# Three changes to the loads of a decode block: where the large tiles lie, how W_o's first heads are split over the DMA engines, and how many pieces W_down comes in

## Chip, cores and metric

The kernel runs on one core of a Trainium2 chip. The metric is the time of one execution on the device, in microseconds. One execution is also profiled; its span runs from the first to the last instruction of the program.

## What is computed

One decode step of a transformer block for B = 2 sequences: layer norm, attention over a cache, and a gated MLP. All tensors are bf16.

```python
D, Hq, Sk, Dh, F = 512, 32, 8192, 128, 1376        # x: [2, 1, 512]
q = layernorm(x) @ wq                              # 32 heads of 128
p = softmax(einsum("bhqd,bhkd->bhqk", q, k_cache) * Dh ** -0.5)
o = einsum("bhqk,bhkd->bhqd", p, v_cache)          # k_cache, v_cache: [2, 32, 8192, 128]
h = x + o.reshape(2, 1, 4096) @ wo
g, u = layernorm(h) @ W_gate, layernorm(h) @ W_up  # [512, 1376]
out = h + (relu(g) * u) @ W_down
```

The caches are 2 x 134 MB and make up nearly all of the 281 MB that are read.

## The kernel before

**Tiles.** Three large buffers (L90, tile0 to tile2) of 64 KB in each of the 128 partitions take turns as K and V tiles. A step (class Step, L130) covers four heads of one sequence: its K tile and its V tile are 8 MB each, loaded by one DMA of 128 rows of 64 KB (load_tile, L160). There are 15 such steps; the last four heads are done as two steps of two heads each (p0, p1), with tiles of half the size. wq lies in half of tile2 at the start. At the end W_o goes into the upper half of tile0 (wo, L125), W_gate and W_up into tile2 (wgu, L126) and W_down into tile1 (wd_sb, L127). The pool `front` stands ahead of the buffers and holds qTs and ocol; all small tiles follow behind them in `consts`.

**A step.** For most of the cache rows DVE multiplies the K tile by q (products, L378) and folds the 128 products of a row in halves (scores, L396, then L398). For the others PE transposes K (L352), ACT copies it back (L353) and PE multiplies by q (L343). DVE finds the maximum (L402 to L417), ACT takes the exponentials (L418), DVE puts them into pgq (L423), and PE multiplies them by the V tile (values, L449).

**Order.** The order on each engine is that of the code (`manual_schedule`). All large loads are issued by SP and go through one queue, which spreads each over the 16 DMA engines; a 128-row load gives every engine 8 rows. A load is issued once its buffer is free, and once the load eight before it has landed, since eight semaphores take turns.

**The end.** After the last full step SP issues V of p0, W_o's first 16 heads (load_set(0), L569, issued from L573), V of p1 in four pieces (L588), W_o's other heads by loads of 8, 4 and 2 heads and the last two (L589 to L594), W_gate and W_up in two pieces each (L614) and W_down (L619). SETS (L68) lists W_o's loads by head: in a load of n heads each partition takes n * D elements in one run. FSETS (L73) does this for W_down by chunks of 128 rows of F: a piece of n chunks gives each partition n * D elements in one run. PE multiplies the heads' output by W_o (attend_set, L505, and attend, L512), then comes the layer norm, then gate and up (through, L673, whose weights are read with a step of n elements in a piece of n chunks), DVE's product (L708), and W_down (L712), chunk by chunk in the order of the loads. The result is transposed (L721), copied (L722) and stored (L723).

Of the kernel before, what the change touches and what calls it, by code (L numbers as in the profile page):

```python
# [13 lines left out]
def _free(t, offset, dims):  # L14

    return bass.AP(tensor=t.tensor, offset=t.offset + offset, ap=[t.ap[0]] + [list(d) for d in dims])


def _dram(t, offset, dims):
    return bass.AP(tensor=t.tensor, offset=t.offset + offset, ap=[list(d) for d in dims])  # L20
# [3 lines left out]
def kernel(  # L24
# [13 lines left out]
    nc = tc.nc  # L38
    P = nc.NUM_PARTITIONS
    B, Sq, D = A_x.shape  # L40
    _, Hkv, Sk, Dh = A_k_cache.shape
    Hq = A_wq.shape[1] // Dh
    F = B_W_gate.shape[1]
# [3 lines left out]
    bf16 = mybir.dt.bfloat16  # L47
    f32 = mybir.dt.float32
# [3 lines left out]
    NQ = Hq // NH  # L52
# [14 lines left out]

    SETS = [(0, 16, 0), (16, 8, 16), (24, 4, 24), (28, 2, 28)]  # L68
    HM = 30
    SROWS = [n for _, n, _ in SETS]  # L70


    FSETS = [(0, 3), (3 * P, 3), (6 * P, 1), (7 * P, 1), (8 * P, 1), (9 * P, 1), (F - P, 1)]  # L73
    FC = 11
    AGAIN = 32

# [3 lines left out]
    front = ctx.enter_context(tc.tile_pool(name="front", bufs=1))  # L80
    big = ctx.enter_context(tc.tile_pool(name="big", bufs=1))
    consts = ctx.enter_context(tc.tile_pool(name="consts", bufs=1))
# [3 lines left out]

    qTs = front.tile([P, B, Hq], bf16)
    ocol = front.tile([P, Hq, B], bf16)

    bufs = [big.tile([P, TILE], bf16, name=f"tile{k}") for k in range(3)]  # L90

# [4 lines left out]
    pv = consts.tile([P, VG * Dh], f32)  # L96
    pick = consts.tile([P, VG, 4, NH], f32)
    zc = consts.tile([P, B, NQ, NH], f32)
    zs = consts.tile([P, B, NQ], f32)
    own = consts.tile([P, NH], f32)  # L100
    ownb = consts.tile([P, NH, VG], bf16)
    ecol = consts.tile([P, TILE // Dh], bf16)
    qzp = consts.tile([P, 2, 16], bf16)
    qz = consts.tile([P, 2 * QZ], bf16)
    ident = consts.tile([P, P], bf16)
    ident_f = consts.tile([QZ, QZ], f32)
# [5 lines left out]
    hm = consts.tile([P, FC, B], bf16)  # L112
    quot = {r: consts.tile([P, Dh // r], bf16, name=f"quot{r}") for r in SROWS}
    rest = {r: consts.tile([P, r], bf16, name=f"rest{r}") for r in SROWS}
    orow = [consts.tile([P, r, B], bf16, name=f"orow{k}") for k, r in enumerate(SROWS)]
    sel = consts.tile([B, B, P // 2], bf16)
# [8 lines left out]
    wo = bufs[0][:, HALF:TILE]  # L125
# [43 lines left out]
    def ln_cols(src, dst_bkc, pfx):  # L169

        m_ps = ps.tile([P, B, KC], f32, tag="mx")
        nc.tensor.matmul(out=m_ps, lhsT=mean_w, rhs=src, start=True, stop=True)
        mean = small.tile([P, B], f32, tag=pfx + "mean")
        nc.vector.tensor_reduce(out=mean, in_=m_ps, axis=AXIS.X, op=ALU.add)
        dev = small.tile([P, B, KC], f32, tag=pfx + "dev")
        nc.vector.tensor_tensor(out=dev, in0=src, in1=_free(mean, 0, [[1, B], [0, KC]]), op=ALU.subtract)
        sq = small.tile([P, B, KC], f32, tag=pfx + "sq")
        nc.vector.tensor_tensor(out=sq, in0=dev, in1=dev, op=ALU.mult)
        v_ps = ps.tile([P, B, KC], f32, tag="mx")
        nc.tensor.matmul(out=v_ps, lhsT=mean_w, rhs=sq, start=True, stop=True)  # L180
        rstd = small.tile([P, B], f32, tag=pfx + "rstd")
        nc.vector.tensor_reduce(out=rstd, in_=v_ps, axis=AXIS.X, op=ALU.add)
        nc.scalar.activation(out=rstd, in_=rstd, func=ACT.Sqrt, bias=eps_col, scale=1.0)
        nc.vector.reciprocal(out=rstd, in_=rstd)
        nc.vector.tensor_tensor(out=dst_bkc, in0=dev, in1=_free(rstd, 0, [[1, B], [0, KC]]), op=ALU.mult)

    with tc.manual_schedule():
# [11 lines left out]
            out=nscale, in_=nscale, compare_op=ALU.not_equal, fill=-SCALE,  # L199
# [5 lines left out]
            out=ident_f, in_=ident_f, compare_op=ALU.not_equal, fill=1.0,  # L205
# [4 lines left out]
            out=sel, in_=sel, compare_op=ALU.not_equal, fill=1.0,  # L210
# [9 lines left out]
            out=pick, in_=pick, compare_op=ALU.not_equal, fill=1.0,  # L220
# [17 lines left out]
        ln_cols(xc, xn.rearrange("p c b -> p b c"), "l1")  # L238
        for r in SROWS:
            nc.vector.tensor_reduce(out=rest[r], in_=_free(ident, 0, [[1, r], [r, P // r]]), axis=AXIS.X, op=ALU.max)  # L240
# [4 lines left out]
        for g0 in range(0, NQ, 4):  # L245
            for n0 in range(NH * g0 * Dh, NH * (g0 + 4) * Dh, 4 * Dh):
                q_ps = ps2.tile([B, 4 * Dh], f32, tag="o")
                for c in range(KC):
                    nc.tensor.matmul(  # L249
                        out=q_ps, lhsT=xn[:, c, :], rhs=wq_sb[:, c, n0:n0 + 4 * Dh], start=(c == 0), stop=(c == KC - 1),  # L250
                    )
                nc.vector.tensor_copy(qrow[:, n0:n0 + 4 * Dh], q_ps)  # L252
            for b in range(B):
                r_ps = ps2.tile([P, 4, Dh], f32, tag="tp")
                for j in range(NH):
                    nc.tensor.matmul(
                        out=r_ps[j * (P // NH):(j + 1) * (P // NH)], lhsT=sel[:, b, 0:P // NH],
# [5 lines left out]
        for j in range(2):  # L263
            nc.tensor.matmul(
                out=r_ps[j * (P // 2):(j + 1) * (P // 2)], lhsT=sel[:, B - 1, :],
# [224 lines left out]
        def lay_rows(k, sps, scalar=False):  # L490

            r = SROWS[k]
            or_ps = ps.tile([P, B, r], f32, tag="mx")
# [7 lines left out]
        def attend_set(k, r0=0, r1=None):  # L501
            for c0 in range(r0, SROWS[k] if r1 is None else r1):
                for c in range(KC):
                    at = (SETS[k][2] + c0) * D + c
                    nc.tensor.matmul(  # L505
                        out=att_ps[:, c, :], lhsT=_free(wo, at, [[KC, P]]), rhs=orow[k][:, c0, :],
                        start=(k == 0 and c0 == 0 and c == 0), stop=False, skip_group_check=True,
                    )

        def attend(h):  # L510
            for c in range(KC):
                nc.tensor.matmul(  # L512
                    out=att_ps[:, c, :], lhsT=_free(wo, h * D + c, [[KC, P]]), rhs=ocol[:, h, :],
                    start=False, stop=(h == Hq - 1), skip_group_check=True,
                )
# [50 lines left out]
        own_sums(Q)  # L566
        def load_set(k):
            h0, n, at = SETS[k]
            nc.sync.dma_start(  # L569
                out=wo[:, at * D:(at + n) * D], in_=_dram(A_wo, h0 * Dh * D, [[n * D, P], [1, n * D]]),  # L570
            )

        load_set(0)  # L573
        products(p0, p0.na)

        at = [0, 0]
# [12 lines left out]
        for k in range(1, len(SETS)):  # L589
            load_set(k)  # L590
        nc.sync.dma_start(
            out=wo[:, HM * D:Hq * D].rearrange("p (h n) -> p h n", n=D),
            in_=_dram(A_wo, HM * Dh * D, [[D, P], [Dh * D, Hq - HM], [1, D]]),
        )  # L594
# [18 lines left out]
        for w, src, c, n in ((0, B_W_gate, 0, 2), (0, B_W_gate, 2, 2), (1, B_W_up, 0, 2), (1, B_W_up, 2, 2)):  # L613
            nc.sync.dma_start(  # L614
                out=wgu[:, w, c:c + n].rearrange("p c f -> p (c f)"), in_=_dram(src, c * F, [[KC * F, P], [1, n * F]]),
            )
        for f0, n in FSETS[-1:] + FSETS[:-1]:
            fc = FC - 1 if f0 == F - P else f0 // P
# [7 lines left out]
            out=z2_ps, lhsT=ones, rhs=_free(zc, ((B - 1) * NQ + groups[Q][1]) * NH, [[1, nb]]), start=True, stop=True,  # L626
# [19 lines left out]
        for k in range(1, len(SETS)):  # L646
            attend_set(k)
        for h in range(HM, Hq):
            attend(h)
# [15 lines left out]

        chunks = [(f0 + c, n) for f0, n in FSETS for c in range(n)]
        UP = 6
# [13 lines left out]
        for c in range(KC):  # L681
# [10 lines left out]
            out=gate, in0=g_ps, scalar=0.0, in1=_free(rvar, 0, [[0, FC], [1, B]]), op0=ALU.max, op1=ALU.mult,  # L692
# [7 lines left out]
        for c in range(KC):  # L700
            nc.tensor.matmul(
                out=d_ps[:, c, :], lhsT=hrow[:, c * P:(c + 1) * P], rhs=ident_f[0:B, 0:B],
# [7 lines left out]
        for fc in order:  # L710
            for c in range(KC):
                nc.tensor.matmul(  # L712
                    out=d_ps[:, c, :], lhsT=wd_sb[:, fc, c * P:(c + 1) * P], rhs=hm[:, fc, :],
# [40 lines left out]
```

## Time and profile before

| | us |
|---|---|
| median of 3 runs | 662.56 |
| lowest and highest of them | 661.42 and 663.75 |
| the profiled execution | 661.14 |
| its span | 659.3 |

The head of the profile gives the busy time of the engines in that span: DVE 557.4 us (85%), PE 353.1 (54%), ACT 122.9 (19%), POOL 7.6 (1%). The 16 DMA engines moved 281.40 MB, 427 GB/s in the mean. "Queue 1" is the one that SP's loads go through; queues 8 and 14 bring instructions. In a row of the timeline the first number is the start in us from the span's start, the second the length; what stands in brackets is the time that the engine had been idle, and what ended it. The chain of waits is the work that ended last, followed backwards from the last instruction. The trace also has a record of each DMA packet, with start, length, size and queue; one row of a load is one packet.

### The profile page before, as it was taken

How to read it: one execution, taken by the hardware profiler on the slowest of the kernel's cores; microseconds unless marked ns; L12 is line 12 of the kernel's file. 1: busy time of each engine (PE TensorE's matmuls, PEld its weight loads, DVE VectorE, ACT ScalarE, POOL GpSimd, SP SyncE). 2: the span in 40 equal slices, each digit the busy share in tenths (PEclk: the TensorE clock that was granted, in tenths of full speed). 3: DMA queues.
4: the chain of work that ended last, by engine and by line, in shares of the span. 5: the costliest groups of instructions: out<-in, count | busy, mean ns of one | idle time of the engine just before them, and what ended most of it. 6: DMA issues, size and time to landing. Idle time of an engine off the chain costs nothing.

```text
span 659.3 us, 5118 instructions
## 1 busy us (share of the span) xinstructions
PE 353.1 (54%) x2123; PEld 160.8 (24%) x2123; DVE 557.4 (85%) x248; ACT 122.9 (19%) x335; POOL 7.6 (1%) x35
## 2 busy tenths in 40 slices
PE   3540924709174480917438092562909358291987
PEld 1220311304022130402214041220403224030456
DVE  2399697989979699997979979896997969999981
ACT  1130030301103020020302102030210304201870
POOL 3000000000000000000000000000000000000010
PEclk9865875959778595977859687695968869686985
DMA  9999999999999999999999999999999999999997
GB/s 382 445 442 445 433 399 441 441 446 434 414 433 430 441 438 421 433 437 426 441 425 434 437 426 433 421 442 437 425 434 427 437 438 425 437 430 412 426 414 279
DMA packets 7946, 281.40 MB, mean 427 GB/s; under 512 B 882, under 2 KB 1780, under 8 KB 2804
## 3 DMA queue, kind: packets, MB, share of 16 engines
q1 hardware_dynamic: 7920, 281.09, 99.0%
q8 instruction: 16, 0.26, 0.2%
q14 instruction: 6, 0.05, 0.0%
q10 hardware_dynamic: 4, 0.00, 0.0%
HBM read 281.09 MB, written 0.00 MB: 426 GB/s over the span
## 4 chain that ended last, share of the span: by engine, by line
DVE 47%; DMA 34%; PE 17%; ACT 1%; issue 1%; SPq 0%; DVEq 0%; ACTq 0%
DMA tile<-in_A_k_cache_dram 28%; DVE tile L378 21%; DVE tile L396 20%; PE pv_ps L449 16%; DMA tile<-in_A_v_cache_dram 3%; DVE scol L398 3%; DMA tile<-in_B_W_up_dram 2%; DVE pgq L423 1%; DMA tile<-in_B_W_down_dram 1%; ACT ecol L418 1%; DVE pm L402 1%; DVE qrep L398 0%; DVE pm L413 0%; DVE hmax L415 0%; PE z_ps L308 0%
## 5 line engine op out<-in xcount | busy, mean ns | idle before, releaser
L449 PE MATMUL pv_ps<-tile,pgq 128*16 128x512 bf16 x960 | 241.8, 417 | 236.4 <-DVE pgq L423 225.0
L378 DVE TENSOR_TENSOR tile<-tile,qrep 128x29696 bf16<-128x29696 bf16 (+3 forms) x16 | 232.4, 14522 | 37.7 <-DMA tile<-in_A_k_cache_dram 37.7
L396 DVE TENSOR_TENSOR tile<-tile 128x14848 bf16<-128x14848 bf16 (+7 forms) x68 | 236.5, 3477 | 2.3
L449 PEld LDWEIGHTS <-pgq 128*16 128x16 bf16 x960 | 91.0, 97 | 376.4 <-DVE pgq L423 235.1
L353 ACT ACTIVATE tile<-t_ps 128x1024 bf16<-128x1024 bf16 x53 | 52.5, 1022 | 18.6 <-PE t_ps L352 18.2
L454 ACT ACTIVATE pv<-pv_ps 16x512 f32<-16x512 f32 (+1 forms) x16 | 9.4, 589 | 234.0 <-PE pv_ps L449 233.9
L418 ACT ACTIVATE ecol<-scol,nmax 128x256 bf16<-128x256 f32 x14 | 7.1, 508 | 196.7 <-DVE nmax L417 196.7
L352 PE MATMUL t_ps<-ident,tile 128*128 128x128 bf16 x424 | 32.7, 230 | 18.1 <-DMA tile<-in_A_k_cache_dram 18.1
L343 PE MATMUL row_ps<-tile,qz 128*24 128x512 bf16 (+1 forms) x98 | 31.0, 399 | 18.6 <-ACT tile L353 18.5
L352 PEld LDWEIGHTS <-tile 128*128 128x128 bf16 x424 | 26.1, 103 | 33.3 <-DMA tile<-in_A_k_cache_dram 18.7
L398 DVE TENSOR_REDUCE scol<-tile 128x232 f32<-128x1856 bf16 (+1 forms) x14 | 28.9, 2067 | 0.5
L423 DVE TENSOR_TENSOR pgq<-ecol,ownb 128x1024 bf16<-128x1024 bf16 x15 | 10.4, 692 | 10.3 <-ACT ecol L418 10.3
L384 ACT ACTIVATE tile<-tile 128x128 bf16<-128x128 bf16 x60 | 17.6, 295 | 1.9 <-DVE tile L378 1.9
L378 DVE TENSOR_TENSOR tile<-tile,qpair 128x4096 bf16<-128x4096 bf16 (+3 forms) x4 | 15.5, 3882 | 0.0
L343 PEld LDWEIGHTS <-qz 128*24 128x24 bf16 (+1 forms) x98 | 7.9, 93 | 28.7 <-issue 23.5
L249 PE MATMUL q_ps<-tile,xn 128*2 128x512 bf16 x32 | 9.7, 469 | 8.4 <-DMA tile<-in_A_wq_dram 8.4
L252 DVE CAST tile<-q_ps 2x512 bf16<-2x512 f32 x8 | 5.4, 678 | 10.2 <-PE q_ps L249 10.2
L370 ACT ACTIVATE scol<-sc_ps 32x24 f32<-32x24 f32 (+1 forms) x56 | 11.7, 209 | 7.7 <-PE sc_ps L365 7.2
L365 PE MATMUL sc_ps<-ident_f,tile 24*128 24x24 f32 (+2 forms) x68 | 7.2, 220 | 11.0 <-ACT tile L361 11.0
L361 ACT ACTIVATE tile<-row_ps 24x512 f32<-24x512 f32 (+2 forms) x17 | 10.0, 586 | 13.4 <-PE row_ps L343 13.4
L312 DVE RECIPROCAL rz<-z_ps 128x16 f32<-128x16 f32 (+1 forms) x4 | 0.9, 236 | 13.1 <-PE z_ps L308 13.1
L384 ACT ACTIVATION_READ_ACCUMULATOR tile<-tile 128x1 f32 x60 | 11.3, 188 | 0.0
(130 smaller groups left out, 132.9 us busy)
## 6 DMA issues: line engine op xcount, KB each, us to landing
tile<-in_A_k_cache_dram SPq DMA_DIRECT2D x2, 4096.0 KB, 22.8
tile<-in_A_wq_dram SPq DMA_DIRECT2D x1, 4096.0 KB, 12.1
tile<-in_A_v_cache_dram SPq DMA_DIRECT2D x1, 4096.0 KB, 19.7
tile<-in_A_v_cache_dram SPq DMA_DIRECT2D x4, 1024.0 KB, 21.0
tile<-in_A_wo_dram SPq DMA_DIRECT2D x1, 2048.0 KB, 24.2
tile<-in_B_W_gate_dram SPq DMA_DIRECT2D x2, 688.0 KB, 13.8
tile<-in_B_W_up_dram SPq DMA_DIRECT2D x2, 688.0 KB, 12.9
tile<-in_A_wo_dram SPq DMA_DIRECT2D x1, 1024.0 KB
```

The costliest lines, as they stand in the source:

```text
L343: nc.tensor.matmul(out=row_ps, lhsT=z, rhs=s.kt[:, (nv + c0 + k) * Dh:(nv + c0 + k + 4) * Dh], start=(u == 0), stop=(u == U - 1),)
L352: nc.tensor.transpose(t_ps[:, k, :], s.kt[:, t * Dh:(t + 1) * Dh], ident)
L353: nc.scalar.activation(out=s.kt[:, (nv + c0) * Dh:(nv + c0 + TPC) * Dh], in_=t_ps.rearrange("p t s -> p (t s)"), func=ACT.Copy,)
L361: nc.scalar.activation(out=rows, in_=row_ps, func=ACT.Copy)
L370: nc.scalar.activation(out=scols[s.i][r, nv:s.nt].rearrange("p (u t) -> p t u", t=4), in_=sc_ps[r, :, :, j], func=ACT.Copy,)
L378: nc.vector.tensor_tensor(out=kv, in0=kv, in1=_free(s.qr, 0, [[0, n], [1, Dh]]), op=ALU.mult)
L384: nc.scalar.activation(out=kv, in_=kv, func=ACT.Copy, accum_out=scols[s.i][:, t:t + 1])
L396: nc.vector.tensor_tensor(out=lo, in0=lo, in1=hi, op=ALU.add)
L398: nc.vector.tensor_reduce(out=scol[:, s.na:s.nv], in_=_free(s.kt, s.na * Dh, [[Dh, s.nv - s.na], [1, 8]]), axis=AXIS.X, op=ALU.add,)
L418: nc.scalar.activation(out=ecol, in_=scols[s.i], func=ACT.Exp, scale=SCALE, bias=nmax, accum_out=zs[:, s.b, s.g:s.g + 1],)
L423: nc.vector.tensor_tensor(out=s.pg, in0=_free(ecol, 0, [[VG, s.nt // VG], [0, NH], [1, VG]]), in1=_free(ownb, 0, [[0, s.nt // VG], [VG, NH ...
L449: nc.tensor.matmul(out=pv_ps[s.i][r, :], lhsT=s.pg[:, u].rearrange("p j t -> p (j t)"), rhs=s.vt[:, u * VG * Dh:(u + 1) * VG * Dh], start= ...
```

## The change

The diff, whole:

```diff
     SETS = [(0, 16, 0), (16, 8, 16), (24, 4, 24), (28, 2, 28)]
     HM = 30
+    P4 = 16
+    LEVEL = 1
     SROWS = [n for _, n, _ in SETS]
...
-    FSETS = [(0, 3), (3 * P, 3), (6 * P, 1), (7 * P, 1), (8 * P, 1), (9 * P, 1), (F - P, 1)]
+    FSETS = [(0, 4), (4 * P, 3), (7 * P, 1), (8 * P, 1), (9 * P, 1), (F - P, 1)]
...
     qTs = front.tile([P, B, Hq], bf16)
     ocol = front.tile([P, Hq, B], bf16)
+    zs = front.tile([P, B, NQ], f32)
+    qzp = front.tile([P, 2, 16], bf16)
...
-    zs = consts.tile([P, B, NQ], f32)
...
-    qzp = consts.tile([P, 2, 16], bf16)
...
         def load_set(k):
             h0, n, at = SETS[k]
+            w = n * D
+            if k < LEVEL:
+                nc.sync.dma_start(
+                    out=wo[0:P4, at * D:(at + n) * D],
+                    in_=_dram(A_wo, h0 * Dh * D, [[P4 // 4 * w, 4], [w, P4 // 4], [1, w]]),
+                )
+            r0 = P4 if k < LEVEL else 0
             nc.sync.dma_start(
-                out=wo[:, at * D:(at + n) * D], in_=_dram(A_wo, h0 * Dh * D, [[n * D, P], [1, n * D]]),
+                out=wo[r0:P, at * D:(at + n) * D], in_=_dram(A_wo, h0 * Dh * D + r0 * w, [[w, P - r0], [1, w]]),
             )
```

It has three parts. The small tiles zs and qzp move into the pool ahead of the three large buffers, which then start 128 bytes further on in each partition, at a multiple of 512 bytes. The load of W_o's first 16 heads becomes two: partitions 0 to 15 by a load whose DRAM side is written as four groups of four rows, and so is spread over four engines, and partitions 16 to 127 by one that all 16 engines share. W_down comes in six pieces instead of seven, of 4, 3, 1, 1, 1 chunks and the last one, where it had 3, 3, 1, 1, 1, 1 and the last one; the last is still loaded first.

## The prediction

> **What bounds the kernel now.** I read the page's head first (spans, queues), then the DVE rows of the timeline from 499 us on, then the PE rows of the tail, then the chain of waits at its end, and last the single DMA packets.
>
> The page: the span, the share in which the 16 DMA engines were busy, and the queues.
>
> ```profile
> span 659.3 us, 5118 instructions
> ...
> DMA  9999999999999999999999999999999999999997
> ...
> q1 hardware_dynamic: 7920, 281.09, 99.0%
> q8 instruction: 16, 0.26, 0.2%
> q14 instruction: 6, 0.05, 0.0%
> ```
>
> The loads never stop: queue 1 alone holds the engines 99.0% of the span. The trace's packet records (start, length and size of each) can be put into sixteen chains, one per engine, by matching each start to an earlier end. On every chain one row follows the other without a gap from 1.75 us to the end of W_down, except where an instruction fetch (q8, 16 KB) stops one engine for about 1.0 us, and makes its next row 0.47 us longer, or a q14 packet stops one for 0.3 us. So the DMA bounds the run, and the engine that had most fetches ends each load last. At the end of W_o's first load the sixteen ends are 627.10, 627.23, 627.32, 627.55, 627.80, then six from 628.38 to 628.84, then five from 629.60 to 629.93: five ahead by 2.1 us or more, five last. W_down's rows end between 652.0 and 655.72.
>
> Is DMA time at the end worth its face? DVE's timeline (start, length, engine, line; in brackets the idle time before and what ended it):
>
> ```profile
> 499.62 15.09 DVE L378 TENSOR_TENSOR tile<-tile,qrep 128x28672 bf16<-128x28672 bf16 x1 [4.19 <-DMA tile<-in_A_k_cache_dram]
> ...
> 538.35 0.26 DVE L312 RECIPROCAL rz<-z_ps 128x16 f32<-128x16 f32 x1 [4.13 <-PE z_ps L308]
> ...
> 573.87 14.55 DVE L378 TENSOR_TENSOR tile<-tile,qrep 128x27648 bf16<-128x27648 bf16 x1
> ...
> 610.53 5.48 DVE L378 TENSOR_TENSOR tile<-tile,qpair 128x10240 bf16<-128x10240 bf16 x1
> ...
> 636.88 0.85 DVE L398 TENSOR_REDUCE qrep<-tile 128x84 f32<-128x672 bf16 x1
> ```
>
> DVE waits for a load for the last time at 499.6 us. From there it works on to 638.1 (131.3 busy of 138.5 us), stopped only by PE and ACT. PE takes over:
>
> ```profile
> 645.36 2.01 PE L505 MATMUL att_ps<-orow,tile 128*128 128x2 bf16 x56
> ...
> 648.94 1.59 PE L673 MATMUL g_ps<-hn,tile 128*128 128x2 bf16 x44 [0.46 <-DVE hn L660]
> ...
> 654.95 1.53 PE L712 MATMUL d_ps<-hm,tile 128*128 128x2 bf16 x44 [0.26 <-DVE hm L708]
> ```
>
> None of its idle times names a load. And the chain of waits, end (start, length, what):
>
> ```profile
> 650.86 5.30 DMA tile<-in_B_W_down_dram
> 656.16 0.05 issue
> 656.21 0.28 PE d_ps L712 x4
> ```
>
> The last four matmuls of L712 start at 656.209; the one before started at 655.989, and they follow each other every 27 ns: PE waited 0.19 us for W_down. So two chains end within 0.2 us of each other: the loads, and compute that hangs on the K tile of 499 us. What the loads win after 499 us is worth 0.19 us at most. What they lose is paid almost in full: W_gate's second piece ends at 648.42, and from W_down the landing is seen 0.44 us after the last row (655.72 to 656.16), so it is there at 648.86, while L673 wants it some 50 ns after 648.94.
>
> **Part 1: tiles at multiples of 512 bytes.** The built program places tile0 at byte 16768 of a partition, 384 past a multiple of 512; zs and qzp (64 bytes each) go in front and make it 16896. Nothing is added on an engine; in the built programs PE, DVE, ACT and POOL have the same instructions in the same order, and only SP's loads differ. A row of 64 KB starts 2414 ns after the one before, one of 8 KB (W_o) after 306, one of 1 KB after 42 to 43. So a byte costs (2414 - 306) / 57344 = 0.03676 ns, and a row has 4.7 to 4.9 ns that do not grow with its size. That surplus is all that alignment could take. Of rows whose tile address differs there are W_gate's and W_up's four pieces, at 384, 256, 128 and 0 bytes past a multiple of 512: all have 207 ns from row to row. Three undisturbed 8 KB packets of q14, an instruction queue that writes no tile, took 309 ns, as most 8 KB rows of V and W_o did. Bounds: nothing, or 4.7 ns a row, 8 + 25 x 8 = 208 rows before the K tile of 499 us, 0.98 us; as a loss, one more such surplus, the same. I take nothing, since the four pieces speak for it.
>
> [...]
>
> **Part 2: W_o's first 16 heads in two loads.** Before, each engine takes 8 rows of 16 KB, 610 ns each. After, partitions 0 to 15 go as 4 x 4 rows through four engines, the other 112 as 7 rows through each: four engines take 11 rows (+1.83 us), twelve take 7 (-0.61). If the four are among those ahead, they end at 627.55 + 1.83 = 629.38 at the latest, the others at 629.93 - 0.61 = 629.32: the last end comes 0.55 earlier, and with it every later load. The chains that started first stayed among those ahead, but no record names an engine. Worth: 0.19 us, the wait of PE; then W_down is no longer late, L712 itself is. If the four are not the ones ahead: +1.83 at worst. The second issue costs SP 0.33 to 0.43 us at 606.2, where it next waits until 611.96, so nothing. Each issue waits for the landing of the eighth before it; with one more in the row, the 8-head load waits for the second K half instead of the first (about 615.6), the 4-head load for V's first half (625.5), and the next two for the two new loads (by 630.4 as now). All run only after 637, so they stay hidden.
>
> **Part 3: W_down in six pieces.** 8 rows of the 56 per engine fall away, and one completion packet: 8 x 4.7 + 9 = 47 ns, inside the 0.19. SP issues one less (0.33 us), and the last piece waits for W_gate's second piece instead of W_up's first, so earlier. PE meets W_gate and W_up with a step of 4 for four chunks, where it had 3 for three: L505, with a step of 4, needs 33 ns a matmul, L712 with none 27, and one more chunk is 8 matmuls: at most 0.05 us. Chunk 3 now comes with chunks 0 to 2, which were there by 653.8, and is wanted after 655.
>
> **Sum.** 0 - 0.19 (parts 2 and 3 together, capped by PE) + 0.05 at most: -0.15 to -0.2 us. The profiled execution took 661.14 us (span 659.3 and 1.8 around it), 1.4 less than the median of the three runs, 662.56. So 660.9 against itself, and 662.4 against the median, which I give. About 0.3% (2 us) is what a measurement of this kernel can tell from no change.
>
> **Rivals.**
> - *The surplus is the address.* The K tile of 499 lands 0.98 earlier, DVE's chain starts as much earlier, the loads end further ahead: -0.98 - 0.19 = -1.2, 661.4. For it: the surplus doesn't grow with the row, as the cost of a bad start would not. Against: 207 ns four times.
> - *Slower: the 112 rows cross.* The sixteen engines take seven consecutive partitions each, so they no longer keep to the partitions that each has in a load of 128. If two engines that write into partitions with a common way into the tile share its rate, a row takes 2 x 0.61. None of seven doubled gives -0.61, all seven +3.66; with five of seven on the last engine it ends 3.05 - 0.61 = 2.4 later, at 632.3, W_gate, W_up and W_down follow, and PE meets each late: 662.56 + 2.4 = 665.0. It decides from the second doubled row on the last engine. Against: x's two 1 KB rows, into neighbouring partitions, overlapped for 27 of their 44 ns and took no longer than W_o's 46; but 1 KB is small. No other load of this kernel writes less than 128 partitions, so the trace can't refuse it. [...]
> - *The wrong four.* The change doesn't do what it says: the four with more rows include one of the five that are last. +1.83: 664.4. For it: the records name no engine, and 16 fetches fell on at least ten chains.
>
> **Chances.** Little change as summed 0.36; address 0.16; crossing 0.30; wrong four 0.12; faster in a way I don't see 0.06. Faster by over 0.3%: 0.10 (the last, and the part of the address rival that profits from more). Slower: 0.42 (crossing, wrong four). Same: 0.48. The range takes the address rival with 0.8 us for the spread of the runs, 660.6, and crossing with seven doubled rows on the last engine, 662.56 + 3.66 = 666.2.
>
> **What would show it.** Alignment: rows of 64 KB at 2409 instead of 2414 ns. Levelling: the spread of the sixteen ends after W_o's first load falls from 2.8 to about 2 us, and no row of 16 KB is much over 613 ns. Crossing: rows of 16 KB near 1.2 us, V's last quarters landing later than 640, and PE waiting for W_gate or W_o in the tail. I am wrong if DVE's wait at 499 moves by more than 1 us, or if PE's rows after 645 begin later by more than 0.5.

## The result, and the profile after

The kernel after takes 668.02 us (median of 4 runs, 667.94 to 668.74), the one before 662.30 (4 runs, with one beside it on the same chip). The ratio is 1.0086 [1.0073, 1.0099]: slower by 5.7 us, above the upper end of the forecast range. The profiled execution took 668.74 us, its span is 666.9, so 7.6 us more than the one shown of before; single executions of the kernel before differ by up to 2.3 us, so the medians carry the size.

The page of after: span, the engines' share, bytes per second in 40 slices, queues.

```profile
span 666.9 us, 5119 instructions
...
DMA  9999999999999999999999999999999999999997
GB/s 377 440 441 440 436 437 440 436 401 430 441 440 433 436 433 428 425 440 441 425 436 437 436 422 436 432 418 436 437 429 433 425 437 436 429 419 430 282 361 282
...
q1 hardware_dynamic: 7792, 281.09, 99.0%
q8 instruction: 16, 0.26, 0.1%
q14 instruction: 6, 0.05, 0.0%
```

The DMA row is all nines as before, so by busy share nothing has happened. The row below tells it: slice 38 (617 to 633 us) moved 282 GB/s and slice 39 361. Before, that row stood at 426 and 414 in these slices (its last slice is low in both kernels):

```profile
GB/s 382 445 442 445 433 399 441 441 446 434 414 433 430 441 438 421 433 437 426 441 425 434 437 426 433 421 442 437 425 434 427 437 438 425 437 430 412 426 414 279
```

The engines are as busy and move less. The windows of after around that place (stretch, length, busy time and count of PE, PEld, DVE, ACT, POOL, clock, DMA share, GB/s):

```profile
499.60:622.00 122.40, 74.79 (x398) 33.05 (x397) 115.75 (x47) 32.06 (x108) 0.00 (x0) 0.80 1.00 432
622.00:639.00 17.00, 14.37 (x70) 5.86 (x70) 15.56 (x12) 12.88 (x67) 1.80 (x1) 0.90 0.98 219
639.00:652.00 13.00, 9.16 (x241) 8.74 (x242) 2.51 (x13) 1.00 (x5) 0.00 (x0) 0.66 1.01 418
```

and those of before:

```profile
499.60:622.00 122.40, 75.34 (x400) 32.95 (x399) 115.52 (x47) 31.83 (x108) 0.00 (x0) 0.80 1.00 431
622.00:639.00 17.00, 15.61 (x140) 8.30 (x137) 16.07 (x13) 13.07 (x67) 2.02 (x1) 1.00 0.99 415
639.00:652.00 13.00, 10.98 (x277) 10.21 (x277) 3.26 (x19) 1.54 (x5) 0.00 (x0) 0.50 1.02 406
```

From 499.6 to 622 us the rates are alike (432 and 431 GB/s), and from 639 on the rate is back (418, before 406). In the 17 us between, while W_o's first 16 heads and V on either side of them are loaded, the rate is half. DVE's last wait for a K tile ends where it did (499.62 before):

```profile
499.89 15.09 DVE L380 TENSOR_TENSOR tile<-tile,qrep 128x28672 bf16<-128x28672 bf16 x1 [4.09 <-DMA tile<-in_A_k_cache_dram]
```

The packet records say which rows. The last column is the time that all rows of a size took, divided by 16: what an engine spends on them in the mean.

| rows | length, before -> after | per engine, before -> after |
|---|---|---|
| 16 KB: W_o's first 16 heads | median 613 -> 1218 ns | 4.91 -> 10.09 us |
| 8 KB: V of p1, W_o's next 8 heads | median of those that start before the last 16 KB row ends 313 -> 582 | 12.59 -> 14.16 |
| 32 KB: V of p0 among them | longest row of V of p0 1707 -> 3205 | 39.58 -> 40.41 |

(The 32 KB rows hold other loads too, whose sum did not change. Over all 8 KB rows the median even falls, from 313 to 309: most of them run behind W_o's first load, and there part 1 evens them out.) The sums, +5.18, +1.57 and +0.83, make 7.6 us, as much as the difference of the two spans. The last W_o row of the first load ends at 638.05 instead of 629.93, the last row of all at 663.36 instead of 655.72.

PE, which in the tail before waited for no load but the 0.19 us for W_down, now waits for V, W_o and W_gate (after; engine, line, releaser, total us, times, longest):

```profile
PE att_ps L507 <- DMA tile<-in_A_wo_dram: 2.2, 2, 1.4
PE pv_ps L451 <- DMA tile<-in_A_v_cache_dram: 1.8, 1, 1.8
PE g_ps L682 <- DMA tile<-in_B_W_gate_dram: 1.4, 1, 1.4
PE o_ps L474 <- DMA tile<-in_A_v_cache_dram: 0.8, 1, 0.8
```

The same in PE's timeline of after:

```profile
629.81 8.59 PE L451 MATMUL pv_ps<-tile,pgp 128*8 128x512 bf16 x32 [1.84 <-DMA tile<-in_A_v_cache_dram]
...
639.14 2.26 PE L507 MATMUL att_ps<-orow,tile 128*128 128x2 bf16 x64 [0.74 <-DMA tile<-in_A_wo_dram]
...
650.97 2.29 PE L507 MATMUL att_ps<-orow,tile 128*128 128x2 bf16 x56 [1.45 <-DMA tile<-in_A_wo_dram]
...
656.85 1.38 PE L682 MATMUL g_ps<-hn,tile 128*128 128x2 bf16 x42 [1.43 <-DMA tile<-in_B_W_gate_dram]
...
662.73 1.31 PE L721 MATMUL d_ps<-hm,tile 128*128 128x2 bf16 x44 [0.26 <-DVE hm L717]
```

The L507 row at 650.97 is the one that began at 645.36 before (L505): 5.6 us later. The other 2.0 us of the 7.6 come behind it, 1.43 of them as the wait for W_gate. The chain of waits of after has its last load further forward than before:

```profile
643.66 13.14 DMA tile<-in_B_W_gate_dram
656.80 0.05 issue
656.85 1.38 PE g_ps L682 x42
```

It is W_gate that ends it now, and W_down (L721) waits for DVE alone: W_down in fewer pieces has no part in the end any more.

### The profile page after: what moved, and what is told of

It is laid out like the page before. It is cut to its first block, busy times and chain, and to the rows that moved or that the text cites. A ratio compares the mean times of both kernels' runs of the same rounds, so it can differ in the third digit from the quotient of the medians.

```text
span 666.9 us, 5119 instructions
## 1 busy us (share of the span) xinstructions
PE 352.0 (53%) x2123; PEld 160.7 (24%) x2123; DVE 557.5 (84%) x248; ACT 123.0 (18%) x335; POOL 7.4 (1%) x35
## 4 chain that ended last, share of the span: by engine, by line
DVE 46%; DMA 35%; PE 17%; ACT 1%; issue 1%; SPq 0%; DVEq 0%; ACTq 0%
DMA tile<-in_A_k_cache_dram 28%; DVE tile L380 21%; DVE tile L398 20%; PE pv_ps L451 16%; DMA tile<-in_A_v_cache_dram 4%; DVE scol L400 2%; DMA tile<-in_B_W_gate_dram 2%; DVE pgq L425 1%; ACT ecol L420 1%; DVE pm L404 1%; DVE qrep L400 0%; DVE pm L415 0%; PE d_ps L710 0%; DVE hmax L417 0%; PE g_ps L682 0%
## 5 line engine op out<-in xcount | busy, mean ns | idle before, releaser
L355 ACT ACTIVATE tile<-t_ps 128x1024 bf16<-128x1024 bf16 x53 | 52.6, 1022 | 17.6 <-PE t_ps L354 17.0
L425 DVE TENSOR_TENSOR pgq<-ecol,ownb 128x1024 bf16<-128x1024 bf16 x15 | 10.4, 692 | 10.3 <-ACT ecol L420 10.3
```

The lines of the kernel that those rows point to most:

```text
L355: nc.scalar.activation(out=s.kt[:, (nv + c0) * Dh:(nv + c0 + TPC) * Dh], in_=t_ps.rearrange("p t s -> p (t s)"), func=ACT.Copy,)
L425: nc.vector.tensor_tensor(out=s.pg, in0=_free(ecol, 0, [[VG, s.nt // VG], [0, NH], [1, VG]]), in1=_free(ownb, 0, [[0, s.nt // VG], [VG, NH ...
```

## The experiments

The theory after the result: part 2 costs all of it, because rows of a load of fewer than 128 partitions are dealt to the engines so that two engines write into the same group of partitions and halve each other. Rivals: the DRAM side of the new loads; the four engines with more rows; the alignment.

### Part 2 alone

The diff's lines on P4, LEVEL and load_set on the kernel before, nothing else.

> The kernel before with the two loads of W_o's first 16 heads alone (part 2). Crossing (engines that write into the same groups of partitions take turns): all of the loss is here, 5 to 6 us more than before, rows of 16 KB near 1.2 us in the middle instead of 0.61. If the new address of the tiles (part 1) made the loss, this one stays within 1 us of before and its rows at 0.61.

Measured: 669.44 us against 661.99, 1.0108 [1.0095, 1.0121]. Rows of 16 KB 1169 ns in the median, and PE waits for W_o and W_gate as in after (and 1.1 us for V):

```profile
PE att_ps L507 <- DMA tile<-in_A_wo_dram: 4.3, 2, 2.8
PE g_ps L682 <- DMA tile<-in_B_W_gate_dram: 1.4, 1, 1.4
```

The whole loss is here: 7.5 us, more than the 5 to 6 that were expected. The interval reaches into that of the three parts together (1.0073 to 1.0099).

### Parts 1 and 3 without part 2

The diff's other lines: zs, qzp and FSETS.

> The changed kernel without the split of W_o's load: parts 1 and 3 alone. If part 2 makes all of the loss: within 0.5 us of before, rows of 64 KB still 2414 ns apart. If the surplus of 4.7 ns a row were the address: rows 2409 ns apart and about 1.2 us faster. If parts 1 or 3 lose: some us slower.

Measured: 661.36 against 661.99, 0.9988 [0.9977, 1.0]. No loss in them; whether a gain is left to the single parts below.

### Two halves of 64 partitions

This takes away the four-engine load and the unequal rows, and keeps a split:

```diff
+            if k == 0:
+                for r0 in (0, P // 2):
+                    nc.sync.dma_start(
+                        out=wo[r0:r0 + P // 2, 0:w], in_=_dram(A_wo, r0 * w, [[w, P // 2], [1, w]]),
+                    )
+                return
```

> The kernel before, W_o's first 16 heads in two loads of partitions 0 to 63 and 64 to 127, all 16 engines in each, no engine with more rows than another. Crossing: 16 engines write into half of the partitions at a time, rows of 16 KB at about 1.2 us in place of 0.61, each half 4.9 us instead of 2.4, 3.5 to 5 us slower in all. If only the unequal number of rows or the four-engine load made the loss: as before within 0.5 us, rows at 0.61.

Measured: 670.27 against 661.99, 1.0114 [1.0098, 1.0131]; rows 1171 ns in the median. The loss stays without any load for four engines, so they are not its cause. It is larger than I had expected (8.3 us, not 3.5 to 5), as PE's waits show (W_o 3.2 us, V 1.7, W_gate 1.4):

```profile
PE att_ps L505 <- DMA tile<-in_A_wo_dram: 3.2, 2, 1.7
PE o_ps L472 <- DMA tile<-in_A_v_cache_dram: 1.7, 2, 1.5
PE g_ps L680 <- DMA tile<-in_B_W_gate_dram: 1.4, 1, 1.4
```

### Seven rows' distance on the DRAM side

One load of 128 partitions as before, but each row starts 112 KB after the one before, as far as an engine's seven rows would put the engines apart. W_o's first 16 heads are replaced by data of the K cache.

```diff
+            if k == 0:
+                nc.sync.dma_start(out=wo[:, 0:w], in_=_dram(A_k_cache, 0, [[7 * w, P], [1, w]]))
+                return
```

> The kernel before, with W_o's first 16 heads loaded by one load of all 128 partitions, but from another place in DRAM: from the K cache, a row of 16 KB every 112 KB, so the first 16 heads of W_o are replaced by other data. Tells the DRAM side from the tile's side. Crossing: no change within 0.5 us, rows at 0.61, since each engine keeps its partitions. If the order in which DRAM is read made the rows slow (engines seven rows apart): rows well over 0.61 and up to 5 us slower.

Measured: 661.82 against 661.99, 0.9999 [0.9990, 1.0008]; rows 613 ns. Its window, to be held beside the 219 GB/s of after:

```profile
622.00:639.00 17.00, 16.81 (x143) 8.33 (x141) 16.69 (x13) 14.42 (x77) 1.61 (x1) 1.00 0.98 411
```

Reading rows 112 KB apart does nothing, so this order on the DRAM side is not the cause. That leaves the tile's side, on which the loads by themselves bear below.

### 32 partitions, by eight engines and by sixteen

Only W_o rows of partitions 0 to 31 are loaded (the other 96 left out), once with the DRAM side written as eight groups of four rows, once as 32 rows:

```diff
+                nc.sync.dma_start(out=wo[0:32, 0:w], in_=_dram(A_wo, 0, [[4 * w, 8], [w, 4], [1, w]]))
```

```diff
+                nc.sync.dma_start(out=wo[0:32, 0:w], in_=_dram(A_wo, 0, [[w, 32], [1, w]]))
```

> The kernel before, but of W_o's first 16 heads only partitions 0 to 31 are loaded (the other 96 are left out), through eight engines with four consecutive partitions each. Crossing, if each engine so keeps to a group of four partitions of its own: rows of 16 KB at 0.61 us, V's rows undisturbed. If any load of fewer than 128 partitions is slow: rows near 1.2.

> The same 32 partitions alone (the other 96 are left out), through all 16 engines with two each. Crossing: twice the engines share the same eight groups, rows of 16 KB at 1.2 us or more, and the next rows of V longer as well; later than the run through eight engines. If engines are what counts: rows at 0.61, two per engine.

Measured, one run each: 662.20 and 662.41 us, rows 1220 and 1202 ns. The first was a miss: 0.61 was expected, and V undisturbed. The two are the same load, so the pair says nothing on eight engines against sixteen. Groups of four adjoining rows are 32 adjoining rows, and in the built program the two dimensions stand merged into one, so both ran on sixteen engines (each has 7824 packets on queue 1: 7920 - 128 - 16 + 32 + 16 completion packets; eight engines would make 7816). What it does show: V's rows of 8 KB, into all 128 partitions, took some 590 ns beside this load instead of 313. The neighbours pay as well.

That led back to the change itself. Its load of 16 partitions, `[[P4 // 4 * w, 4], [w, P4 // 4], [1, w]]` with P4 // 4 = 4, is merged in the same way into 16 rows, and goes through **sixteen** engines, one row each. The page confirms it, since a load brings one completion packet per engine it uses (16 behind a 128-row load, 4 behind the load of 4 rows below, which has four rows in flight at once). Part 2 alone:

```profile
q1 hardware_dynamic: 7936, 281.09, 99.0%
```

16 more than before, not 4. So by these packets every engine had 1 + 7 = 8 rows, as before the change, and nothing was levelled.

### Loads by themselves

Behind the output's store, thirteen loads of 16 KB rows were added to the kernel before, each waiting for the last (only these added loads matter; the 741.53 us hold them).

```diff
+        for r0, n, dims in (
+            (0, 128, [[w, 128]]), (0, 64, [[w, 64]]), (0, 32, [[4 * w, 8], [w, 4]]), (0, 32, [[w, 32]]),
+            (0, 16, [[4 * w, 4], [w, 4]]), (0, 16, [[w, 16]]), (0, 128, [[8 * w, 16], [w, 8]]), (16, 112, [[w, 112]]),
...
+            (0, 4, [[w, 4]]),
+        ):
+            nc.sync.dma_start(out=bufs[0][r0:r0 + n, 0:w], in_=_dram(A_wo, r0 * w, dims + [[1, w]]))
```

> The kernel before with thirteen more loads of W_o rows of 16 KB behind its output store, each waiting for the landing of the one before, into a part of tile0 that nothing reads any more: rows by form of load with nothing else in flight. Crossing in groups of four partitions and those 32 further, consecutive partitions per engine: 128 partitions 0.61 us a row; 64 partitions, even 0 to 63 or 64 to 127, 1.2; 32 through eight engines by four 0.61; 32 through 16 engines 1.2; 16 through four engines by four 0.61; 16 through 16 engines 2.4; 112 between 0.61 and 1.8; 4 partitions through four engines 2.4. If every load of fewer than 128 partitions is slow by itself: all but the 128s alike. If only loads that meet other loads are slow: all 0.61.

Measured, row median and length of the load: 128 partitions 611 ns and 6.2 us; 112 (16 to 127) 934 ns and 8.0 us; 64 partitions 1272 and 5.0; 32 partitions 1022 and 2.4; 16 partitions 1244 and 1.7; 4 partitions 783 and 0.9. Written as groups that merge, the load is the same: 128 partitions as 16 groups of 8 take 611 ns, 16 as 4 groups of 4 take 1329 with 16 completion packets. The 112 rows that the change loads take 1.5 times as long as 128's with nothing else on the queue (934 against 611 ns). Two expectations failed: 16 rows through 16 engines and 4 rows through four were to take 2.4 us a row, on the guess that four engines in one group of four partitions share one rate. They took 1.2 to 1.3 and 0.8, and the runs don't show why.

### Four engines in earnest

Part 2 with groups that can't merge, since a gap of four rows lies between them on the DRAM side. Partitions 4 to 15 get other rows of W_o in it.

```diff
-                    in_=_dram(A_wo, h0 * Dh * D, [[P4 // 4 * w, 4], [w, P4 // 4], [1, w]]),
+                    in_=_dram(A_wo, h0 * Dh * D, [[2 * P4 // 4 * w, 4], [w, P4 // 4], [1, w]]),
```

> Part 2 alone, as it was meant. In the built program the DRAM side of the 16-partition load, four groups of four adjoining rows, had been merged into 16 rows, and the thirteen-load run showed one row on each of 16 engines. Here the four groups lie twice as far apart in DRAM, so they can't be merged; partitions 4 to 15 so get other rows of W_o than they should. If the merging made the loss (no levelling, 16 engines in the same place): about as fast as before, 662 us. If crossing in the 112-row load makes it: rows still near 1.2 us, 4 to 8 us slower than before.

Measured: 670.44 against 662.40, 1.0119 [1.0098, 1.0141]. Now four engines are used, as the page shows (4 more than 7920):

```profile
q1 hardware_dynamic: 7924, 281.09, 98.9%
```

and the 16 KB rows still take 1195 ns. So the merging did not make the loss: the split as it was meant loses 8.0 us here.

### How partitions are dealt

Nine loads by themselves as above, now with groups that can't merge, so that each engine takes one group of consecutive partitions.

```diff
+            (0, 128, [[w, 128]]), (0, 32, [[8 * w, 8], [w, 4]]), (0, 16, [[8 * w, 4], [w, 4]]),
+            (0, 64, [[16 * w, 8], [w, 8]]), (0, 64, [[8 * w, 16], [w, 4]]), (0, 128, [[16 * w, 16], [w, 8]]),
+            (0, 128, [[32 * w, 8], [w, 16]]), (0, 32, [[4 * w, 16], [w, 2]]), (0, 128, [[w, 128]]),
```

> Nine loads behind the output store again, each alone, with DRAM sides that can't be merged, so that the number of engines is as written (the rows are others of W_o, nothing reads them). If engines write at full rate as long as no other engine is in their group of four consecutive partitions or the one 32 further: 32 partitions through eight engines 0.61 us a row, 16 through four 0.61, 64 through eight engines by eight 1.2 (engines 0 and 4 in the same groups), 128 through 16 engines, eight consecutive rows each, 1.2 if the partitions are dealt as written, 0.61 if the split of a 128-partition load is always the same. If a load through fewer partitions is slow whatever the engines: 1.0 to 1.3 for all under 128.

| partitions, engines x consecutive partitions | row median | load |
|---|---|---|
| 128, plain | 611 ns | 6.4 us |
| 128, 16 x 8 | 1276 | 10.4 |
| 128, 8 x 16 | 1238 | 19.5 |
| 64, 16 x 4 | 1225 | 5.4 |
| 64, 8 x 8 | 1265 | 9.9 |
| 32, 16 x 2 | 1100 | 2.8 |
| 32, 8 x 4 | 611 | 3.3 |
| 16, 4 x 4 | 611 | 3.3 |

Each load was run once; each had 16, 8 or 4 completion packets, as written. It is not the number of partitions: 32 run at 611 ns by 8 x 4 and 16 by 4 x 4, while 128 take 611 or 1276 through 16 engines, by how they are dealt. One engine to every four consecutive partitions (0 to 3, 4 to 7, up to 31) took 611 ns a row (8 x 4), as in the plain load. With two engines in every four partitions a row took 1100 (16 x 2). With no two engines in the same four by the forms as written, but 64 partitions in use, so that each engine has another 32 partitions further, it took 1225 (16 x 4) and 1265 (8 x 8, where only eight engines run at all). These rows fit the groups of the expectation, four partitions together with those 32 further; no form tests the distance of 32 against others, and none shows what makes the groups. That a plain load of 128 is dealt so that this does not happen is inferred from its 611 ns.

The forms differ on the DRAM side too, where the engines' blocks lie 64 to 512 KB apart. That distance alone is not the cause: 128 KB apart, rows take 611 ns by 8 x 4 and 1225 by 16 x 4, and the plain loads of 64 and 112, whose rows adjoin in DRAM as those of 128 do, are slow.

### Part 1 alone

The moves of zs and qzp (tile0 from byte 16768 to 16896).

> The kernel before with part 1 alone. In the run of parts 1 and 3 the shortest rows did not change (2418 ns for 64 KB) but nearly all rows had that length, where before more than half were 1 to 11 ns longer. If the address does this: the same here, 64 KB rows in the mean some 1.5 ns shorter than before (0.4 us per engine over the run), 8 KB rows 309 in nearly all cases, 0.5 to 1 us faster. If not the address but W_down's pieces: as before.

Measured: 660.56 us (12 runs, 659.63 to 663.47) against 662.15 (23 runs), 0.9983 [0.9971, 0.9995]. It beats both kernels, by a margin that only many runs show. DVE's last K wait ends 0.44 us sooner than the 499.62 of before, which by itself shows nothing: in the four profiles with tiles at multiples of 256 that row starts between 499.18 and 499.89, in the ten others between 499.53 and 501.56.

```profile
499.18 15.09 DVE L378 TENSOR_TENSOR tile<-tile,qrep 128x28672 bf16<-128x28672 bf16 x1 [4.08 <-DMA tile<-in_A_k_cache_dram]
```

The most usual lengths are what they were (2418 ns for 64 KB, 309 for 8 KB). But before only 45% of the 64 KB rows took no more than 2418 ns, and most of the others 1 to 11 more; now it is 90%. This does hold from profile to profile: 42 to 63% in the ten with tiles as before, 88 to 91% in the four at multiples of 256. The mean of 64 KB rows under 2.5 us falls from 2420.6 to 2419.6, of 8 KB rows from 314.7 to 310.2, of 4 KB from 160.9 to 159.0. With 240 rows of 64 KB per engine at 1.0 ns less, 40 of 8 KB at 4.5 and the small ones, that is some 0.5 us per engine, as the sum over all rows of queue 1 also gives (653.05 to 652.55 us per engine). The medians give 1.6 us, with an interval of 0.3 to 1.9 from the ratio, so the rows explain the lower part of it.

A row's own tile address does not decide it alone. After the change, W_gate's and W_up's second pieces start 128 bytes past a multiple of 256, by the kernel's offsets both in the tile and in their DRAM tensors. Yet all 512 rows of the four pieces took 211 ns there, where 78% did before. Before, tile and DRAM offsets of these pieces, and of the K and V loads, differed by 128 within 256 bytes; after, they agree. The runs fit this, but none tests it by itself.

### A multiple of 256 only

ocol moved behind the buffers, which puts tile0 at byte 16640, 256 past a multiple of 512.

```diff
-    ocol = front.tile([P, Hq, B], bf16)
...
+    ocol = consts.tile([P, Hq, B], bf16)
```

> The kernel before with ocol moved behind the large tiles, so that they start at 256 past a multiple of 512 bytes, where they were at 384 and part 1 has them at 0. If a multiple of 256 is what makes the rows even: some 90% of the 64 KB rows at 2418 ns or less, as with part 1. If it must be 512: 45 to 61%, as in the runs with tiles at 384.

Measured, one run: 660.51 us beside 662.70; 90% of the 64 KB rows at 2418 ns or less, 8 KB rows 310.2 in the mean, as with a multiple of 512. The step from 128 to 256 bytes has the gain, by the rows; one time does not prove it. Another small tile was moved here than in part 1, so the places of zs and qzp are not the cause.

### Part 3 alone

FSETS alone.

> The kernel before with part 3 alone, W_down in six pieces. If the address made the rows even: rows as uneven as before, and the time within 0.3 us of before. If the pieces did: rows even and 0.5 to 1 us faster.

Measured: 662.15 against 662.15, 0.9994 [0.9984, 1.0004]. Nothing, as foretold. The rows stay uneven: 61% of the 64 KB rows at 2418 ns or less.

## Why the prediction was wrong

- **The bound was read rightly.** Loads never stop, and what they lose after 499 us is paid nearly in full: +7.6 us of engine time per engine became +7.6 of span.
- **Part 2, the step that failed:** "partitions 0 to 15 go as 4 x 4 rows through four engines, the other 112 as 7 rows through each: four engines take 11 rows (+1.83 us), twelve take 7 (-0.61)". By the completion packets no engine had 11 or 7 rows: each had 8. I took the four groups from the diff, and the built program has them merged. But the term that counts is the price, 610 ns a row, which was carried over from a load of 128 partitions to loads of 16 and 112. The 16 KB rows took 1218 ns, and with the four engines that the step assumed still 1195, for a loss of 8.0 us.
- **The crossing rival had the effect**, as far as the loads by themselves show it: 611 ns a row for 8 x 4, 1100 for 16 x 2, 1225 for 64 partitions by 16 x 4. Its common way into the tile, and the seven consecutive partitions for each engine, were my guess: no run shows the first as such, and in the change's own loads no record says which engine took which partitions. Its three signs came: 16 KB rows near 1.2 us, V late (PE waits for its last quarter until 648.50; the last 8 KB row of V and W_o ends at 650.55, before at 642.38), PE waiting for W_gate and W_o. What was mis-sized is its term "five of seven doubled", 2.4 us, with "all seven", 3.66, as the end of the range. The 16 KB rows alone cost 5.18: the 16-row load, one of 8 rows on each engine, is slow too (1244 ns by itself), and rows reach 1828 ns, three times 610. The other 2.4 us (1.57 + 0.83) lie in V's and W_o's full loads before and behind. The sum left them out: I priced the load that was changed, and not what runs beside it while the engines are up to 2.8 us apart. That the neighbours are slowed is shown (with 32 rows they took 590 ns). That the spread of the engines lets them overlap is argued.
- **Its chance**, 0.30 against 0.36, I kept below that of the sum for the sake of two 1 KB rows of x. In the loads alone, the smallest kept most of their rate too (four rows of 16 KB 783 ns, where full loads have 611), so such rows could not speak for long ones. Whether levelling between engines can gain at all is not shown: four engines in earnest gave 1.0119, with the slow 112-row load in it.
- **The wrong four** fell: there were no four, and with four in earnest the loss was 8.0 us, not 1.83, with slow 16 KB rows.
- **Part 1** I put at nothing, and it is worth 0.17% (0.05 to 0.29). The four pieces of W_gate and W_up spoke rightly against the address rival: in the most usual rows the 4.7 ns surplus does not go with the address (2418 ns for 64 KB and 309 for 8 KB before and with part 1 alone). But I had read rows by their most usual value (309 ns for 8 KB, which only 29% of them had), and the gain lies in the mean, in extras of some ns that in this profile came on more than half of the 64 KB rows. The address rival took 4.7 ns off each row; the rows give 1.0 ns on those of 64 KB, 4.5 on those of 8 KB. Why only some rows have extras stays open.
- **Part 3** was right.
- Part 2 (1.0108) and part 1 (0.9983) multiply to 1.0091, with part 3 (0.9994) to 1.0085, against 1.0086 [1.0073, 1.0099] measured: within the intervals the parts add up.

Open: which engine takes which partitions of a load of 112 or 128, since no record names an engine, and why four engines in one group of four partitions, one row each, are so little slowed. A split by columns with all 128 partitions in each load wasn't tried, nor whether any other levelling gains.

## What to carry to other kernels

Don't split a large load by partitions without trying it: here 128 rows in one load took some 611 ns each, in two loads about twice that, and the full loads on either side lost time with them. A DMA share that stays at 0.98 while GB/s halves (415 to 219) is the sign. Read how many engines a load uses from the built program or its completion packets (16, not 4, here, as the adjoining groups had been merged). Judge alignment by the mean row, not by the most usual one.

## What the runs showed of the hardware that I had not expected

- Two forms of a 2 MB load of 128 partitions by 16 engines took 611 and 1276 ns a row.
- A load of only 32 rows slowed rows of other loads on the same queue from 313 to some 590 ns.
- Four rows of 16 KB into partitions 0 to 3 by four engines took 783 ns, only 1.3 times a row of a full load, while sixteen rows into partitions 0 to 15 took 1244.
- With the large tiles at 128 past a multiple of 256, rows of 8 KB took 314.7 ns in the mean, with the tiles at multiples of 256 310.2, with the same shortest row of 309.
